# Key buffers of the first batch four deep, half of them in the channel mix's room, with a new order of issue

## The chip, the cores and the metric

One core of a Trainium2 chip runs the whole program. The metric is the time of one execution in device microseconds. The five engines (TensorE or PE, VectorE or DVE, ScalarE or ACT, GpSimd or POOL, SyncE or SP) run their own instruction lists side by side and wait for each other by semaphores; SP's list here is the queue from which all loads, copies and transposes by DMA are issued.

## What is computed

Attention with queries averaged over pairs, then a channel mix (shifted blend, squared ReLU, sigmoid gate) over the attention's output. Shapes: batch 8, heads 8, 1152 keys, head size 64; d_model 512, d_ff 1024.

```python
q_pool = q.reshape(B, H, S // 2, 2, D).mean(axis=3)
scores = scale * np.matmul(q_pool, k.transpose(0, 1, 3, 2))
attn = softmax(scores)                                  # max subtracted, over the keys
x = np.matmul(attn, v).transpose(0, 2, 1, 3).reshape(B, S // 2, H * D)
x_prev = shift(x, 1)                                    # one token back in the sequence
xk = mu_k * x + (1 - mu_k) * x_prev
xr = mu_r * x + (1 - mu_r) * x_prev
out = sigmoid(xr @ w_r) * (np.maximum(xk @ w_k, 0.0) ** 2 @ w_v)
```

## The kernel before, in words

There are 64 heads n (batch n//8, head n%8), and each head's 576 pooled queries are worked on in 6 blocks of 96, so 384 blocks i with n = i//6. All numbers are split into a high and a low half of 16 bits, and products are summed from the halves.

A head's keys take this way (`prep`). They are loaded into kr (L453). ACT makes their high half in kn (L474), POOL the low half (L479; DVE for the first two heads). A transpose by DMA turns kn into ks1, with the high half in partitions 0 to 63 and the low half in 64 to 127 (L482). A copy by DMA then brings ks1's high half to partitions 64 to 127 of ks2 (L485). The other half of ks2 is constant, and set once by memsets at the start (L395, L396). There are two buffers each of kr, kn, ks1 and ks2, taken in turn (n%2). Head 0 is done on PE instead of by transposes. Queries are loaded two heads at a time (L418) and turned by two DMA transposes, one for the high and one for the low half (L443). Values are loaded into vr (L453).

A block is worked on like this (`block`). Nine matmuls of ks1 with the queries' high half (L526, *first scores*) go into a PSUM buffer, s[i%3]. DVE takes the maximum of each query over its nine tiles (L548, *long max*); a matmul with the identity, identb, transposes the result (L551); DVE takes the maximum again (L559, *short max*). In the first 60 blocks a matmul spreads this over the block (L563). ACT writes the negative into a row of the queries' low half (L540). Nine matmuls of ks2 with it (L531, *second scores*) add the low part and subtract the maximum. ACT takes the exponential (L573), POOL makes its low half pl (L535), and PE sums values with it (L613 to L620).

After a batch's 48 blocks its 576 tokens go through the channel mix in tiles of 256 (`ff`): matmuls (L827), ReLU (L854), Square into g32 (L856), its low half gl by POOL (L858), more matmuls, the gate, and the store. The weights are loaded (L706) and split into halves beside the first batch. g32 and gl lie idle until the first tile's Square.

Each engine's order is not the order of the code. Every operation is recorded with what it reads and writes, and at the end `Issue.run` takes, engine by engine, the next operation from the list by a number of a packed table, TURNS. `Issue.gaps` adds spare matmuls of zeros on PE in the early part (L960). The order that results is fixed; the engines still wait for data and free buffers.

Of the kernel before, what the change touches and what calls it, by code (L numbers as in the profile page):

```python
# [13 lines left out]
F32 = mybir.dt.float32  # L14
F16 = mybir.dt.float16
# [40 lines left out]
    "Wp$1da!`$gsp`6(3h1tz<nXvoOyz)@N-}EMwk0EzFde=Qmd!rd&{ad#RR%C9a^e6fEG{>d%VjhwD3wYLr4ky;jZMu>C^t0LDYf<WwRLr<Rq7k+mHK+rwbvC2"
    "g<=tfT)sA6Q&)qUn%Wv<3)y@olg$>hl|oTrgF-r;OQ$o7G8v?E%7SdZkk96F$z&#(P9ixqnN3d0C~7*BMoO)VCX$J0A|8#UBT76OPZC#3FdB`<qQPJ|IK2|="
    "sB~A<PNm|yZd;q%+UmN^s$w^{*-iD$<rbi+mVH2@Q7jee8_hCGjSYIC9_&p{WF}%usfJ>zl&VXmYSOioIR(UXxwx9hqzzToGg>T?N@^SyEgo^Axo9Y&go#(h"
    "a1Fx_$#m+v6OhmtkYvaV2F-w+lX@Uv8;)b>mP`dSTazhV7`5%NY6UG0yB6qDyE;`fpth-MTYFnG6s4(2Yf>6ZC^d5;8XM72wu*&PsiwZZVAR$Yp%?0MT1`!{"
    "uGp$5@JF;hmCR<7$#foxDad5fYAVyO+Ny?lFvj_hgcXN!0#0a#Md3_07-T*G-E~4Chw_@P9%!NXuI@Mvv14*P*(;ISA*$@9nibHXI<{&_HmX`yNHqzhUR86t"  # L60
    "y0lJHH7W#9v)a<42b!7;wXxJ7J!ooTCmQO}(AZF%S_`$VR;{h+*HA#JCY3HCUz1-@ET#*od{QtlT+D!pY$BaTCYw>yM#@mb@wgsSlfhs-9)zld5ecf{kP-||"
    "2nH?14IAACyI{CM_J?Lgx)2J5PPFtu$Or{FH=HUO20dUN%1S$6i)~?7*a6p^6;ZVr)3xCl>XGWOI*p@csFNp~lP9Ta|KQ|)b<#vADs`f_zq7v&TDzvVR-m+_"
    "t*xzdr<O_u9i5$>?R!@$EtL+@m6i^4v^S^??S|T<*Xn9xqY6#Y)EX3X>3lww$`&g{_Lw-Mx+K}z9F?P{m@1@-lZv^*Ag42x&n1y5B#=*J)l5!{Wiq<1E>9X-"
    "+(0y{I^np&tLcQJ3+)KaS142+fiA17(^^*P>h1!i>a=Jdy4v(grMaV1@2r$79h9-XrCjN(pb3?>29dP2Rn-l>Tvn|j2RGYT1C;6&ic~kXE>l~}X&Oiu3aM1C"
    "rY2KN)fP}JCJV{@?0i01n@gtHhrHzTKsK9-$J42fR8Ea&v~)~Y6IwEsNT{J$3<0W*f>_WO--^&a2NwsGATj7T^Cvk+OwuP9gT@4Xa8Mr{(EIg1y?1bMu)C|P"
    "Zvg1;>+h>ndNj4G-|Dm+&D2z*thcpxw5la~o~9;?n$pl(ER}S%uCbV-cB{j=TuohFT~?{7QPB^Io6M%DEcsNfFrOXbT;y_)p--gpMHCC!LS7~GG&P-%Y2j=}"
    "*Mec_$(Rz4Q*|Ovn4q&wCG3Vx!weEsRH9H2Of7IH>65GpmOj8f4DQ4(^y+$FuRho#qVG{rd-~MAUaQkkwMvWH-qGHq8JbQr+M>2JEA<MBC0bTZRa&8CYijb@"
    "VnNN<qLvzhDK*Jlp)g2+3;9g0CRtNNE#)OPGC78%8jIy)NtM<#s$`OCI;E<KfWQM0*zpkkLc~$Qo(M$5GU<BA5fh+0)OOdQ$FWUa2h?iNG*xp|O}Ch~RVbQ5"
    "uRwtK0j92L@bj*2SBoU?2Tgvu??i@n8j>(`XlQq)6bwz7I#pGsOrAVRqdHCC#41X^GKj%}fq|)02L^ik`+NIlp;zha>Fw@8cel!kpV_5!cA}@!-O)9%t7~?5"
    "S4U@u(xITet*y0<utiG?TAG`crg=)aJXmgN)XHj^<JgGS270Xe+WNZMTA*gv+M4}p2?A;ziurtgI);aLnK?WISxn1}Ov6xmXzG+HsxmQ&iHZIRgX#bV(HrfH"  # L70
    "_ICC5^r+nkqoPjh0$M8_E$uGaowhch#cD1oN~8EjO>3wx>Gd@Vlwz)iiYqQIry!F`r?M#(DJ6+SB3c*cC7)<dMB)k+Vjvm^LXk+2CpR1pghHULswF*g#b$+6"
    "Ql)_KAcYe|zhRI?*n_;xWP($mYbpWL($b<dD=p~aNT8`v0{wHjv8SP->^qN!dImJqLEN2O&|DBVSK>6~v&eRccTP{pWGH<SDUmUeK)gAgibbP+aZu7|JkDz<"
    "nk1$oh;)a-!BD%nL2)Zi0CW<ti71nzj{6IJx@9?*z0j}>p(wLSP;|2!26=@hbJwc2DN2hnO&mnImGU<FM5CcRt%*`kZd4i?6l!*D2_k)|Sl>eFQ9BC|et}%J"
    "O*lj*lk1a#R?>-7DupDS24bWO@nmOG`hjpPHV{i75{reSVtZQIg8)^5Lma`1uuI<;h8t9*4<?<$fwoJAMAikv+EYYk7&eWa^r0bOiaJ%9GDVrZe6j#pnShBq"
    "Pn?Je0}}^8MDK!u$pZuEA4CtezK5sYJ}}jVS)Fb45*?lGm9`E*4h1vHEzJ!>O%3HX_M3xHDskTE%^MnOOB4N0E2Ub6^ooQ^sli~e*iYY}AeT#L3z@vYD-VGf"
# [203 lines left out]
def kernel(  # L279
# [40 lines left out]
    def bufs(name, n, shape, dt):  # L320
        return [const.tile(shape, dt, name=f"{name}{i}") for i in range(n)]
# [679 lines left out]
```

## Time and profile before

| | us |
|---|---|
| median of 3 runs (lowest, highest) | 1079.94 (1078.45, 1080.11) |
| profiled execution | 1079.3 |
| its span | 1077.5 |
| PE busy | 1054.2 (98%) |
| DVE busy | 891.2 (83%) |
| ACT busy | 781.0 (72%) |
| POOL busy | 750.1 (70%) |

The granted clock is 1.0 over the span. The busy share of PE counts matmuls with modelled ends, so 98% isn't PE at its peak. The stretch that the key buffers belong to is the first batch, about the first 104 us. The trace's waits are listed by the line that waits and the line that released it; a wait of SP's queue is one of the DMA behind it in the list.

### The profile page before, as it was taken

To read this page: it belongs to the slowest core of one execution; us is meant where nothing else is said; L and a number is where in the kernel's file an instruction comes from. 1 tells how busy PE (TensorE), PEld (TensorE's weight loads), DVE (VectorE), ACT (ScalarE), POOL (GpSimd) and SP (SyncE) were. 2 spreads that over 40 slices of the span, in tenths; PEclk is the share of its full clock that TensorE was granted. 3 is DMA by queue.
4 is the path that set the end of the run, shared out by engine and by line. 5 is a ranking of instruction groups with operands and counts; after the bars stand their busy time and mean duration, and the time that the engine had idled before them with its cause. 6 is when DMAs were issued, how large, how long until landed. Compare 5 with 4: busy or idle time off the path is not lost.

```text
span 1077.5 us, 38432 instructions
## 1 busy us (share of the span) xinstructions
PE 1054.2 (98%) x16153; PEld 867.3 (80%) x16153; DVE 891.2 (83%) x1609; ACT 781.0 (72%) x1523; POOL 750.1 (70%) x748
## 2 busy tenths in 40 slices
PE   8999999999999999999999999999999999999998
PEld 7888878879698888978687978788887879796665
DVE  8999999898978989788779888897988798886331
ACT  7988987777687776777667777777787777665333
POOL 5676778877689676876586886868677876765321
PEclk9999999999999999999999999999999999999999
DMA  9999766764747666665446556547563983521001
GB/s 234 215 241 199 168 166 125 168 131 106 165 94 137 129 128 135 129 127 115 123 95 150 111 115 145 127 94 134 123 155 63 171 157 86 98 47 36 11 20 40
DMA packets 257772, 134.94 MB, mean 125 GB/s; under 512 B 192960, under 2 KB 230080, under 8 KB 257600
## 3 DMA queue, kind: packets, MB, share of 16 engines
q1 hardware_dynamic: 257600, 132.49, 58.2%
q8 instruction: 126, 2.06, 0.8%
q14 instruction: 46, 0.38, 0.1%
HBM read 67.11 MB, written 9.44 MB: 71 GB/s over the span
## 4 chain that ended last, share of the span: by engine, by line
PE 80%; DVE 7%; issue 1%; DMA 1%; POOL 0%; ACT 0%; DVEq 0%; POOLq 0%; ACTq 0%
PE f L827 34%; PE a L613 12%; PE s L526 11%; PE s L531 11%; PE a L620 5%; PE s L827 5%; DVE mx L548 3%; PE s L551 2%; PE a L827 2%; DMA st<-st 1%; DVE mx L559 1%; DVE raw L644 0%; DVE xk L776 0%; DVE xr L776 0%; DVE ex L882 0%
## 5 line engine op out<-in xcount | busy, mean ns | idle before, releaser
L535 POOL TENSOR_SCALAR pl<-pf 128x864 f16<-128x864 uint16 (+1 forms) x384 | 353.7, 921 | 165.3 <-ACT pf L573 135.3
L548 DVE TENSOR_REDUCE mx<-s 128x96 f16<-128x864 f32 x384 | 402.8, 1053 | 53.2 <-PE s L526 31.5
L573 ACT ACTIVATE pf<-s 128x864 int32<-128x864 f32 x384 | 339.7, 888 | 122.7 <-PE s L531 97.7
L613 PE MATMUL a<-vt,pf 128*128 128x129 f16 x2520 | 255.6, 220 | 0.3 <-DVE raw L640 0.3
L531 PE MATMUL s<-qT,ks 128*128 128x96 f16 x3456 | 234.0, 206 | 2.7 <-DMA ks<-ks 1.2
L526 PE MATMUL s<-qT,ks 128*128 128x96 f16 x3456 | 233.7, 206 | 2.3 <-ACT pf L573 1.2
L526 PEld LDWEIGHTS <-ks 128*128 128x128 f16 x3456 | 191.3, 98 | 32.6 <-issue 4.4
L531 PEld LDWEIGHTS <-ks 128*128 128x128 f16 x3456 | 186.4, 98 | 24.3 <-issue 2.2
L620 PE MATMUL a<-vb,pl 128*128 128x65 f16 x2376 | 202.1, 193 | 0.6 <-POOL pl L535 0.6
L613 PEld LDWEIGHTS <-pf 128*128 128x128 f16 x2520 | 176.5, 98 | 27.2 <-issue 0.4
L620 PEld LDWEIGHTS <-pl 128*128 128x128 f16 x2376 | 144.0, 99 | 0.8 <-POOL pl L535 0.8
L540 ACT ACTIVATE qT<-s 1x96 f16<-1x96 f32 x384 | 90.4, 235 | 74.5 <-PE s L551 61.0
L827 PE MATMUL f<-xlk,wk_hi 128*128 128x256 f16 x496 | 135.2, 272 | 0.0
L827 PE MATMUL f<-xhk,wk_lo 128*128 128x256 f16 x496 | 135.1, 272 | 0.0
L827 PE MATMUL f<-xhk,wk_hi 128*128 128x256 f16 x496 | 135.1, 272 | 0.0
L559 DVE TENSOR_REDUCE mx<-s 128x1 f16<-128x128 f32 x324 | 92.8, 286 | 48.3 <-ACT qT L540 46.1
L827 PEld LDWEIGHTS <-wk_hi 128*128 128x128 f16 x1152 | 104.7, 98 | 13.9
L858 POOL TENSOR_TENSOR gl<-g 128x512 f16<-128x512 f32 x72 | 78.4, 1093 | 49.2 <-ACT g L856 46.8
L827 PE MATMUL f<-wv_hi,g 128*128 128x512 f16 (+1 forms) x248 | 92.4, 374 | 1.4 <-ACT em L877 1.4
L479 POOL TENSOR_TENSOR kn<-kr,kn 128x576 f16<-128x576 f32 x62 | 83.7, 1351 | 13.3 <-ACT kn L474 9.7
L827 PE MATMUL f<-wv_hi,gl 128*128 128x512 f16 (+1 forms) x248 | 92.4, 374 | 0.0
L827 PE MATMUL f<-wv_lo,g 128*128 128x512 f16 (+1 forms) x248 | 92.4, 374 | 0.0
(127 smaller groups left out, 1887.3 us busy)
## 6 DMA issues: line engine op xcount, KB each, us to landing
kr<-in_k_dram SPq DMA_DIRECT2D x64, 288.0 KB, 3.5
vr<-in_v_dram SPq DMA_DIRECT2D x64, 288.0 KB, 3.6
qr<-in_q_dram SPq DMA_DIRECT2D x31, 576.0 KB, 5.6
ks<-ks SPq DMA_DIRECT2D x64, 144.0 KB, 3.1
out_dram<-em SPq DMA_DIRECT2D x35, 256.0 KB, 3.4
xt<-in_moe_w_v_dram SPq DMA_DIRECT2D x8, 512.0 KB, 4.7
st<-in_moe_w_k_dram SPq DMA_DIRECT2D x4, 512.0 KB, 6.0
xt<-in_moe_w_k_dram SPq DMA_DIRECT2D x4, 512.0 KB, 6.7
```

Source lines behind the costliest of these rows:

```text
L479: lambda cs=cs, en=nc.vector if ve else nc.gpsimd: en.tensor_tensor(kn[i][:, cs, D:P], kr[i][:, cs], kn[i][:, cs, 0:D], op=ALU.subtract),
L526: nc.tensor.matmul(cols(c, c + 1), ks1[hp][:, c, :], qhi, start=(c == c0), stop=False, skip_group_check=True)
L531: nc.tensor.matmul(cols(c, c + 1), ks2[hp][:, c, :], qlo, start=False, stop=True, skip_group_check=True)
L535: op("POOL", 0.917 if buf == ("pside",) else NC * (r1 - r0) / 1200 + 0.27, lambda: nc.gpsimd.tensor_scalar(to, half(pf, U16, 0)[:, :, HALF ...
L540: op("ACT", 0.131, lambda: nc.scalar.activation(qlo[0:1], src, AF.Prelu, scale=scale, alpha=(1.0 + EPS) / (1.0 - EPS)), r=[("s", at)] + kl ...
L548: op("DVE", 0.974, lambda: nc.vector.tensor_reduce(mxz[:, P - QN:P], grid(0, NC).rearrange("p c q -> p q c"), axis=AX.X, op=ALU.max), r=[( ...
L559: op("DVE", 0.199, lambda: nc.vector.tensor_reduce(to, s[:, 0:P], axis=AX.X, op=ALU.max), r=[("s", z), ("row", z)], w=[("col", z1) if join ...
L573: op("ACT", NC * QN / 1200 + 0.067, lambda: nc.scalar.activation(pf[:, :, HALF + rows.start:HALF + rows.stop], grid(0, NC), AF.Exp, bias=S ...
L613: nc.tensor.matmul(u[:, k_], hi, vt[jv][:, c, 0:D + VN], start=(head and c == 0), stop=last, skip_group_check=True)
L620: nc.tensor.matmul(sum_, pl[:, c, rows], vb[jv][:, c, 0:VN], start=False, stop=(c == NC - 1), skip_group_check=True)
L827: nc.tensor.matmul(ps, terms[i][0], terms[i][1], start=(first and i == 0), stop=(i == last), skip_group_check=True)
L858: op("POOL", 2 * n * 0.0018 + 0.186, lambda f2=f2: nc.gpsimd.tensor_tensor(gl[:, f2, 0:n], g32[:, f2, 0:n], gh[:, f2, 0:n], op=ALU.subtrac ...
```

## The change

In the first batch (n < 8) ks1 and ks2 rotate over four buffers each; from head 8 on over two, as before. The two new ks1 and one new ks2 are parts of g32, read as 16 bit numbers; the other new ks2 is a part of gl. The first tile's Square and its low half are recorded as writing these buffers, so they wait for the last scores that read them. The fixed half of the two new ks2 is set by memsets on POOL, which are operations of the ordered list. The buffers kr, kn, vr and the queries' buffers are as before. The table TURNS is replaced as a whole, so that all five lists change; they hold the same operations but for POOL's memsets and the spare matmuls (98 before, 106 now).

```diff
 TURNS = (
-    "c-nP(2bdhi)$QpVCg-?ec4zZ!-c?+*iYOpJLTiEmArK$~GQogZi~*CQjlf1EVZi)gO!5!b17i$Yg28}DCW)Lxd<X;*0+ISZw`a}wzW2UYHQimQyKhyUd+(|0"
...
+    "c-nP(d7xd>z5i#=!<py#p7EYLoI8(6?#(D6lPRts9)g-<tZ=C*TC;NNp-)AUqMjP6NGs+j^@vLiC26!sL|bV?h!BMRK5L)ouYdgB+Gp>**4k^Yy@t>C^Zl&7"
...
@@ -369,6 +369,17 @@
     g32 = const.tile([P, NF, T], F32, name="g32")
     gl = const.tile([P, NF, T], F16, name="gl")
     r32 = bufs("r32", 2, [P, 2, T], F32)
+    room = [g32.rearrange("p f t -> p (f t)").bitcast(F16)[:, o * NC * P:(o + 1) * NC * P] for o in range(3)]
+    room.append(gl.rearrange("p f t -> p (f t)")[:, 0:NC * P])
+    early_k = [x.rearrange("p (c x) -> p c x", c=NC) for x in room]
+    ks1 += early_k[0::2]
+    ks2 += early_k[1::2]
+    borrowed = [[("ks1", 2, c) for c in (0, 4, 8)] + [("ks2", 2)] + [("ks1", 3, c) for c in (0, 4, 8)], [("ks2", 3)]]
+
+    def slot(n):
+
+        return n % 4 if n < H else n % 2
...
-    for t_ in ks2:
-        nc.vector.memset(t_[0:D], 0.0)
-        nc.vector.memset(t_[0:1].bitcast(F32), SM2)
+    def fixed(t_, en):
+        en.memset(t_[0:D], 0.0)
+        en.memset(t_[0:1].bitcast(F32), SM2)
+
+    for i_, t_ in enumerate(ks2):
+        if i_ < 2:
+            fixed(t_, nc.vector)
+        else:
+            op("POOL", 1.3, lambda t_=t_: fixed(t_, nc.gpsimd), w=[("ks2", i_)], key=-100.0)
...
-            op("DMA", 1.91, lambda: nc.sync.dma_start_transpose(ks1[i], kn[i].rearrange("p c x -> p (c x)")),
-               r=[(m, i, 0) for m in ("kn", "knl")], w=[("ks1", i, c) for c in (0, 4, 8)],
+            op("DMA", 1.91, lambda: nc.sync.dma_start_transpose(ks1[m], kn[i].rearrange("p c x -> p (c x)")),
+               r=[(x, i, 0) for x in ("kn", "knl")], w=[("ks1", m, c) for c in (0, 4, 8)],
                key=key + 1, tail=1.53)
-        op("DMA", 0.95, lambda: nc.sync.dma_start(ks2[i][D:P], ks1[i][0:D]),
-           r=[("ks1", i, c) if n else ("ks1h", c) for c in (0, 4, 8)], w=[("ks2", i)], key=key + 1, tail=1.57)
+        op("DMA", 0.95, lambda: nc.sync.dma_start(ks2[m][D:P], ks1[m][0:D]),
+           r=[("ks1", m, c) if n else ("ks1h", c) for c in (0, 4, 8)], w=[("ks2", m)], key=key + 1, tail=1.57)
...
-                nc.tensor.matmul(cols(c, c + 1), ks1[hp][:, c, :], qhi,
+                nc.tensor.matmul(cols(c, c + 1), ks1[kz][:, c, :], qhi,
...
-                nc.tensor.matmul(cols(c, c + 1), ks2[hp][:, c, :], qlo,
+                nc.tensor.matmul(cols(c, c + 1), ks2[kz][:, c, :], qlo,
...
-                g32[:, f2, 0:n], r32[z][:, :, 0:n], AF.Square), r=[("r32", z)], w=[("g", f0)], key=key + 1)
+                g32[:, f2, 0:n], r32[z][:, :, 0:n], AF.Square), r=[("r32", z)], w=[("g", f0)] + (borrowed[0] if t0 == 0 else []), key=key + 1)
...
-               r=[("g", f0)], w=[("gl", f0)], key=key + 1)
+               r=[("g", f0)], w=[("gl", f0)] + (borrowed[1] if t0 == 0 else []), key=key + 1)
```

Three places of the new order matter below. The lines of the changed kernel have other numbers: L453, L482, L485 and L443 are L470, L499, L502 and L460 there.

The first is SP's list at head 4, whose keys go through kn0 and ks1_0; qT0 is the queries of heads 4 and 5, xt2 a weight's piece. Before:

```order
L482 DMA_TRANSPOSE ks1_0_81<-kn0_79 128x9x128
L453 DMA kr0_73<-in_k_dram 128x576
L706 DMA xt2_110<-in_moe_w_k_dram 128x1024
L443 DMA_TRANSPOSE qT0_85<-qn0_69 128x9x128
L418 DMA qr0_77<-in_q_dram 128x9x128
L443 DMA_TRANSPOSE qT0_85<-qn0_69 128x9x128
L453 DMA vr0_75<-in_v_dram 128x576
L485 DMA ks2_0_83<-ks1_0_81 64x1152
```

And in the changed kernel:

```order
L460 DMA_TRANSPOSE qT0_85<-qn0_69 128x9x128
L435 DMA qr0_77<-in_q_dram 128x9x128
L499 DMA_TRANSPOSE ks1_0_81<-kn0_79 128x9x128
L470 DMA kr0_73<-in_k_dram 128x576
L470 DMA vr0_75<-in_v_dram 128x576
L460 DMA_TRANSPOSE qT0_85<-qn0_69 128x9x128
L502 DMA ks2_0_83<-ks1_0_81 64x1152
```

The weight's piece is gone from between the transpose (first row before) and the copy (last row), and the first query transpose and the query load stand ahead of both.

The second is SP's list at the change from head 7 (kn1, ks1_1; in the changed kernel the parts of g32 and gl) to head 8 (kn0, ks1_0). Before:

```order
L482 DMA_TRANSPOSE ks1_1_82<-kn1_80 128x9x128
L453 DMA kr0_73<-in_k_dram 128x576
L453 DMA kr1_74<-in_k_dram 128x576
L706 DMA xt2_110<-in_moe_w_r_dram 128x1024
L485 DMA ks2_1_84<-ks1_1_82 64x1152
L418 DMA qr0_77<-in_q_dram 128x9x128
L482 DMA_TRANSPOSE ks1_0_81<-kn0_79 128x9x128
```

And in the changed kernel, after head 7's transpose:

```order
L723 DMA xt2_110<-in_moe_w_r_dram 128x1024
L499 DMA_TRANSPOSE ks1_0_81<-kn0_79 128x9x128
L723 DMA xt2_110<-in_moe_w_r_dram 128x1024
L470 DMA kr0_73<-in_k_dram 128x576
L470 DMA kr1_74<-in_k_dram 128x576
L502 DMA ks2_0_83<-ks1_0_81 64x1152
L502 DMA gl_117<-g32_116 64x1152
```

Head 7's copy (the row into ks2_1 before, the row into gl now) has moved behind head 8's transpose and head 8's copy.

The third is POOL's list at the start. Before:

```order
L343 MEMSET qn0_69 128x9x64
masks.py:199 ISA
masks.py:199 AFFINE_SELECT ident_63<-ident_63 128x128
L345 TENSOR_SCALAR negi_71<-ident_63 128x128
L341 CAST identb_68<-ident_63 128x128
```

And in the changed kernel:

```order
masks.py:199 AFFINE_SELECT ident_63<-ident_63 128x128
L406 MEMSET gl_117 64x1152
L345 TENSOR_SCALAR negi_71<-ident_63 128x128
L407 MEMSET gl_117 1x576
L406 MEMSET g32_116 64x1152
L407 MEMSET g32_116 1x576
L341 CAST identb_68<-ident_63 128x128
```

All four new memsets stand ahead of identb, the identity that PE's first transposes read.

## Rows read from the trace of the kernel before

**Rows 1.** The page, busy time of the whole span, and the chain that ended last, by engine.

```profile
PE 1054.2 (98%) x16153; PEld 867.3 (80%) x16153; DVE 891.2 (83%) x1609; ACT 781.0 (72%) x1523; POOL 750.1 (70%) x748
...
PE 80%; DVE 7%; issue 1%; DMA 1%; POOL 0%; ACT 0%; DVEq 0%; POOLq 0%; ACTq 0%
```

**Rows 2.** Busy time by stretch (us from the start, length, then each engine; clock, DMA share, GB/s).

```profile
25.00:50.00 25.00, 23.31 (x567) 21.64 (x564) 23.32 (x42) 22.45 (x43) 16.64 (x18) 1.00 1.09 208
75.00:106.00 31.00, 28.58 (x655) 26.02 (x655) 29.99 (x54) 27.08 (x51) 21.17 (x21) 1.00 1.00 206
```

**Rows 3.** All waits of VectorE, 9 to 106 us (line waited for: us in total, times, longest).

```profile
DVE mb L559 <- PE s L551: 2.0, 4, 1.0
DVE mx L548 <- PE s L526: 1.3, 3, 0.9
DVE mb L559 <- PE s L960: 0.7, 2, 0.4
DVE mx L548 <- ACT qT L540: 0.6, 1, 0.6
```

**Rows 4.** Waits of TensorE, 175 us to the end: the two on maxima.

```profile
PE s L551 <- DVE mx L559: 1.9, 3, 1.1
PE s L551 <- DVE mx L548: 1.5, 3, 0.9
```

**Rows 5.** Waits of TensorE, 0 to 106 us: the one kind on key transfers.

```profile
PE s L531 <- DMA ks<-ks: 1.2, 2, 1.0
```

**Rows 6.** Timeline of TensorE at block 24 (start, length, what, [idle before <-releaser]).

```profile
58.32 0.56 PE L531 MATMUL s<-qT,ks 128*128 128x96 f16 x9 [1.03 <-DMA ks<-ks]
```

**Rows 7.** Timeline of VectorE behind this wait.

```profile
58.97 0.29 DVE L559 TENSOR_REDUCE mb<-s 128x1 f16<-128x128 f32 x1 [0.97 <-PE s L551]
```

**Rows 8.** Wait of SyncE's queue for TensorE, 38.5 to 42.2 us.

```profile
SPq L482 <- PE s L526: 2.7, 1, 2.7
```

**Rows 9.** Timeline of SyncE's queue, head 4's transpose to head 4's copy.

```profile
41.88 1.32 SPq L482 DMA_TRANSPOSE ks<-kn  x1
...
47.62 5.32 SPq L443 DMA_TRANSPOSE qT<-qn  x1
...
53.66 0.47 SPq L485 DMA_DIRECT2D ks<-ks  x1
```

**Rows 10.** Landings of L485's nine key copies, then of L482's nine key transposes, 0 to 106 us.

```profile
DMA to landing us min/median/max: 2.9/5.3/7.1
...
DMA to landing us min/median/max: 3.4/5.3/8.8
```

**Rows 11.** Timeline of GpSimd at the start.

```profile
0.87 0.58 POOL L343 MEMSET qn<- 128x576 f16 x1
...
2.21 0.29 POOL L341 CAST identb<-ident 128x128 f16<-128x128 f32 x1
```

**Rows 12.** Timeline of TensorE at its first use of identb.

```profile
6.38 0.54 PE L436 MATMUL s<-identb,qn 128*128 128x128 f16 x5
```

**Rows 13.** Timeline of VectorE at the start.

```profile
1.20 1.14 DVE L395 MEMSET ks<- 64x576 uint32 x2
```

**Rows 14.** Timeline of TensorE at the last second scores of head 7.

```profile
103.48 0.37 PE L531 MATMUL s<-qT,ks 128*128 128x96 f16 x5
```

**Rows 15.** Timeline of ScalarE at the first Square.

```profile
120.52 0.61 ACT L856 ACTIVATE g<-r 128x512 f32<-128x512 f32 x1
```

**Rows 16.** Timeline of SyncE's queue, head 7's copy and head 8's transpose.

```profile
84.60 0.47 SPq L485 DMA_DIRECT2D ks<-ks  x1
...
87.35 4.21 SPq L482 DMA_TRANSPOSE ks<-kn  x1
```

**Rows 17.** Timeline of GpSimd, low halves of head 8's keys.

```profile
80.68 1.69 POOL L479 TENSOR_TENSOR kn<-kr,kn 128x576 f16<-128x576 f32 x1
```

**Rows 18.** Timeline of TensorE, first second scores of head 7.

```profile
94.71 0.54 PE L531 MATMUL s<-qT,ks 128*128 128x96 f16 x9
```

**Rows 19.** Landing of head 7's copy, issued at 84.60.

```profile
DMA to landing us min/median/max: 6.8/6.8/6.8
```

More of the change, by code (lines that the diff above doesn't have):

```diff
@@ L56 @@
[L56 to L63, printed above, removed]
@@ new lines @@
+    "Y)Pi1>6#Yi%|^)5bv+f(t+1{_hY?C^x~!#CLzOj6)*`y9sj{82<e()Ra==7X*P!ZQ-7qp{(9m_&Fanm!NB}uaG1QpCXKQ&as`(W)s2~~k*&bMulrrp;5%$0g"
+    "m?G$@xNe&8TNaG0t@~I}*tFEBu4fWiRrB~ffNfhD*)(OZY<XfH)AWjlo0<^_8!(L^TW<1}lmSBz_=6l<C1S@Cw%7L9io(vxAroQSG!h&i7LBs7W#+wxs#`h~"
+    "-3;l9t}7vURE0%7VbhikQ`UW!&HMaDSd6O`_UNW+u#0>q2Uq8;$ucB&V~|xzfht!TD{{Fkp~z4w7ONGM8>@||l*&>=v7ykA&qK-;N(HG<K)yB8kjZ4T$fVK@"
+    ">0Cb7fLuck*<>b}NF|ayOPLlH$i(BRcsy}HB7t~Hnwv~#(#cdR8cjsw(aAAHlhFxMT#hH=h{^eAEEtIf!@*EIAcdphXv80ur69o+^m_f?Hg9cmTW6cpF16XV"
@@ new lines @@
+    "-O|$9VmEtiSu(3FRkKi)n)1~W*awueB`s4xsiGFuVljh!F<mGm^2r9Uh4D;7p;(B=V!3=AxmXrRr^B(Z9FHritR|FDJQjc~p&=5q!w4c6uso92YXm$24L;4Q"
+    "YPMG;qCI8JwpGjL^Qk(sG><3Z^=O7=X{zB-J+=zZfhIWfnql~5U6%uz(j|AA9e!D>ar9e_))rZ=pwW=ZQmKS|fg=sD2gQ6T%NfWN3JrRLRs=fpc^Sw?b8K!l"
+    "8!u*J>1Z@M6`5!(8BHJ@lcVt-Sym#DwV)IX*os7(L%=rKx`1x@e7e^=pnE)op6T^^HQ1`B$;&>Nwyjw-E03q%1)^0^M3X(rLRgj}vp<&T13O^bdXHD_>QXzc"
+    "E?boqKF}vOHC3v5qg<(!P-;T83IeKta-m$x%7t8dFrCwKSt2bZWf9Ayo7363>;YrZ=!{e{nayQmu_!>!h$RxT9E+)eNJI|D6@oepPf$Y058bc(Y&O4Nv_U6%"
@@ new lines @@
+    "u%W6Y2HCa=YT8s*_j=Ctu(!78ie@p>d!p*mXey@7j&L3fF$b15!#`b_rc9kKpC(U}r?3~6JaOW{#0iRw-o6RSgh7b`J?KSmPg{3Q>ulB3wl<}!)*?5xp@zn`"
+    "mj1R{bEUQApw^a31+^+lEzPA8r;=l$l*&p`Mpl(+81ZyEO{>V&V)2XsS|*uJ$2f8E_!My|ni3h&6aylOOpQ2{Q<3zES}G-n60)j9)u_)GQer`lX((hEmOm&3"
+    "bid^HX&iy+n%$uu-QG@eYi-lmq*`mORnwZ=)LKn#t<)GQt*xz<N~Nj7D}+{Slibo=Y;MvNQ>~PtWF%EB=fr%)8nTIOLxSiUh-KYoBFSmWWO7Zp+?*UkA|6dQ"
+    "5P)%ZC5}is9Z9E1i;4C`CYp}QNhPet5^^LK3#t*t8&cp2_}OZ&6)^p#FL1CK@RRS|nbRx`3=HV~GX{0FU+wGb>sEVu7OCC+YDaG`divVMv8T63snzt39uBIe"
@@ new lines @@
+    "wyUbQA~)BXRiz-Ku~9;$+)~b!GQ~_KSI(3&nZnePQY>mxK0lbx3r=IJa`8+w6HCR|ABLIf7-=V)$YhX?W+D*d9#2NXaXFUK<b)QNbwqqpL<)y_Ke?DJPR!}L"
+    "LBK(nI_*UjfV0#=Q&s!>W~jaW1EL3$R8{Tn?&$9V8@`~Yt+%U3>6VQa4s@-`v4`4BPgZVjX_ghKk+YdA%h^&<K~p|YR@%EERZNmnrDRTOh;xjyu_RL6WJ$7U"
+    "hA_%TW8iS7l95Cr98b$yQcoyBHA>Emc_okAVA7P|3@Ju{p2-&o1SG%V(`gkFhufojXy$CZCVYo3+$w|vP-ImVN5wEzkraNG?iK8g#oeHHS0pkI<F@K%$Z#D-"
+    "-D$W!gKlK*WK13w;lSZxMkEYR8XA&^q=^%y2`o9#-!J#kn)=bt$sQi!g!lG#OWiZj)!E(I)djhu10C({?bF)PR_m;FbPRTM%<Sx_wb!(oB(=7*5Vp<DO-)Te"
@@ L127 @@
+    "=&VV6_OOGjm38Wdi$_5WlCDU!9EG(?b*%6Cm@Phkxbgo5o%%Fl"
 )
@@ L450, in prep @@
         b, h = divmod(n, H)
-        i, j = n % 2, n % NV
+        i, j, m = n % 2, n % NV, slot(n)
         def dma(o, src, buf, late=0.0):
@@ L506, in block @@
     def block(n, j, i, t):
-        hp, z = n % 2, i % 3
+        hp, z, kz = n % 2, i % 3, slot(n)
         qi = n // 2 % 2
@@ L546, in front @@
                 op("PE", (c1 - c0) * 0.0425, lambda c0=c0, c1=c1: scores(c0, c1),
-                   r=[("ks1", hp, c) for c in (0, 4, 8) if c0 <= c < c1] + kh, w=[("s", z)], key=t)
+                   r=[("ks1", kz, c) for c in (0, 4, 8) if c0 <= c < c1] + kh, w=[("s", z)], key=t)
             op("DVE", 0.974, lambda: nc.vector.tensor_reduce(mxz[:, P - QN:P], grid(0, NC).rearrange("p c q -> p q c"),
@@ L571, in back @@
                 op("PE", (c1 - c0) * 0.0425, lambda c0=c0, c1=c1: scores2(c0, c1),
-                   r=[("ks2", hp)] + kl, w=[("s", z)], key=t + O_EXP)
+                   r=[("ks2", kz)] + kl, w=[("s", z)], key=t + O_EXP)
             op("ACT", NC * QN / 1200 + 0.067, lambda: nc.scalar.activation(
```

123 lines of the change are left out of this document (57 added, 66 removed).

## Prediction, made before the changed kernel was run

> **What bounds the kernel now.** I read first the busy times and the chain of waits, then the busy time of each engine by stretch, then each engine's list of waits in the stretches that the change touches, then the timelines around single waits. The profiled execution took 1079.3 us, 0.64 below the median of the three runs (1079.94). Two of a thousand, 2.16 us, is about what a measurement of this kernel can tell from no change.
>
> Over the whole span TensorE is busy 98%, and 80% of the chain runs over it [rows 1]. That is an average of two stages. From 25 to 50 us DVE and PE are busy alike, 23.3 of 25; from 75 to 106 DVE is busy 29.99 of 31 us and PE 28.58 [rows 2]. So the first batch (blocks 0 to 47, until about 104 us) runs at the pace of VectorE's maxima, and an engine that is late there costs time only if it makes DVE wait. All that DVE waits for between 9 and 106 us adds up to 2.0 + 1.3 + 0.7 + 0.6 = 4.6 us [rows 3]. **This is the ceiling of what new key buffers can give in the first batch.** After it the kernel runs at PE's pace, and PE's waits for maxima there are 1.9 + 1.5 = 3.4 us over 900 us [rows 4].
>
> **The change part by part.**
>
> *1. Heads 2 and 4: the copies ks1 to ks2 come in time.* These are the only key transfers that PE waits for: 1.2 us in two waits [rows 5], 1.03 of them before block 24 [rows 6] and the rest before block 12. The second goes on to DVE, which stands 0.97 us for the transposed maxima behind it [rows 7]; so 1.03 of PE are 0.97 of the bound engine. Why head 4 is late: its transpose into ks1[0] must wait until head 2's last scores have read that buffer (2.7 us of SyncE's queue on PE [rows 8]); it issues at 41.88, and its copy, seven rows behind it, at 53.66, after a query transpose that holds the queue 5.32 us [rows 9]. With slot n%4, head 4 goes into the buffer that head 0 left, so the wait of 2.7 us goes, and the list now puts the copy four rows behind the transpose: of what stood between them, a query load and the first of two query transposes come ahead of both, a weight load goes elsewhere, and the second query transpose stays between. Without the 2.7 alone the copy can issue up to 2.7 us earlier, and it needs 1.03. I take -1.2; bounds 0 (the queue takes the time back) and -1.2 (all of it).
>
> *2. The fixed parts of two more ks2.* Four memsets come onto POOL ahead of identb. The nearest row of POOL is 0.58 us for 576 elements a partition [rows 11]: the two of 1152 cost 2 x 1.16, the two of 576 cost 2 x 0.58, together 3.48 us. identb ends at 2.50 before, at about 5.98 now; PE first reads it at 6.38 [rows 11, 12]. It is hidden by 0.40 us of POOL's idle time, so 0. At DVE's price (two wide pieces in 1.14 [rows 13], so four in 2.28) the margin would be 1.6; if POOL's went by bytes (4 x 1.16) PE would start 0.76 late. Bounds 0 and +0.8.
>
> *3. The room.* Two ks1 and one ks2 lie in g32, the other ks2 in gl, so the first Square of the channel mix and the first gl wait for the scores of heads 2, 3, 6 and 7. The last of these run at 103.48 [rows 14]; the first Square is at 120.52 [rows 15]. 17 us lie between, so 0, and no bound.
>
> *4. Head 7's copy moves the other way.* Before, it stood right behind two key loads and a weight load, and issued at 84.60 [rows 16]. Now it stands behind head 8's transpose and head 8's copy. Head 8's keys are turned only after POOL has their low halves, 80.68 + 1.69 = 82.37 [rows 17]. A transpose lands after 5.3 us at the median, 8.8 at most, and a copy after 5.3, 7.1 at most [rows 10]. At the medians head 8's copy issues at 87.7, head 7's at about 88.2, and it lands at 93.5. PE wants it at 94.71 [rows 18], or 93.5 if term 1 holds. I take 0; the other end is the slowest landings, 82.4 + 8.8 + 0.5 + 7.1 = 98.8, so +5.3.
>
> *5. The order everywhere else.* Each engine's list is new, but with the same operations. On DVE the maxima keep their pace, and in several places of the first batch a short max now precedes a filler (a weight's or a value's piece) that it followed. What this can work on is the 3.4 us of DVE's waits that are left beside term 1 (4.6 - 1.2), and PE's 3.4 after the first batch. Of the latter the largest, 1.1 [rows 4], would move, not go: at block 102 the new list puts the short max ahead of the next long max instead of behind it, so that one is 1.05 us later. I take a third of the first 3.4 and none of the second: -1.1. Bounds: -4.5 (all of the first, a third of the second) and +2, as two waits as long as block 24's come up at places that were tuned in the old list.
>
> The sum: -1.2 + 0 + 0 + 0 - 1.1 = -2.3. From 1079.3 that is 1077.0, and with the 0.64 between profile and median **1077.6 us**.
>
> **The rivals.**
>
> *A. The change does not deliver (1079.0).* The copies come earlier in the list, but SP's queue is what it was: 16 DMA engines are kept busy all through the first batch (share 1.09 and 1.00 [rows 2]), the query transpose that holds the queue 5.32 us still stands ahead of head 4's copy, and the kernel is bound by DVE, where single waits removed come back at the next max. For it: DVE's waits are already under 5% of the stretch. Against it: head 4's transpose loses a definite wait of 2.7. Then terms 1 and 5 give half of 1.2 and about a third of the last: -0.9, so 1079.0, which is no change that can be told.
>
> *B. Head 7's copy becomes the wait (1082.2).* PE would stand at block 42's second scores, and DVE behind it as at block 24. With head 8's transpose landing as late as the slowest (82.4 + 8.8 = 91.2) and head 7's copy at the median (91.7 + 5.3 = 97.0), PE waits 97.0 - 93.5 = 3.5 us: 1079.94 - 1.2 + 3.5 = 1082.2. It decides from 1.2 + 2.16 = 3.4 us of waiting, when head 8's transpose takes over 8.7 us to land, or the copy from 88.2 over 8.7. For it: head 8's transpose stood 4.21 us in the queue before, and head 7's copy took 6.8 to land, over its median [rows 16, 19]; two weight loads now stand on either side of that transpose. Against it: the median landings just fit, and in the list before PE had 3.3 us to spare (84.60 + 6.8 against 94.71). From these rows, one landing of this copy known and slow, one in about five: 0.18.
>
> The Trainium skill (DMA: Bandwidth & Descriptors, section "Queues, rings and completion order") says that a DMA's semaphore write is held until all earlier writes of that DMA engine have landed, those of other queues too. By that rule a copy of 144 KB lands as late as the loads ahead of it, the slowest landings would be the usual ones here, PE would wait 98.8 - 93.5 = 5.3 us, and the time would be 1084.0; that copies land after 5.3 us at the median but after 2.9 at the least [rows 10] agrees with it in part only.
>
> *C. More than that (1073.8).* DVE's waits go altogether (4.6) and 1.5 of PE's after it: 1079.94 - 6.1 = 1073.8. Against it: the list must then be right at every place.
>
> **How the numbers follow.** The forecast has a chance of 0.40 and C 0.06, both faster: 0.46. A has 0.36. B has 0.18, with a late start of PE (part 2) on top in some of it. The predicted time is the forecast's, 1077.6. The range starts at C, 1073.8, and goes up over A to B's own figure, 1082.2. Left out are about half of C (0.03) and the heavier half of B (0.09). Faster than 1077.8 (1079.94 - 2.16) is 0.46; up to 1082.1 (1079.94 + 2.16) it is A's 0.36; slower is B's 0.18.
>
> **What would show it.** Right: no wait of PE on the copy at heads 2 and 4, and none of SP's transposes waiting for PE's scores before 100 us; DVE's waits from 9 to 106 us at some 2.3 us instead of 4.6; the first batch ends about 2 us earlier and the rest runs as long as before. Wrong: a PE wait on the copy at head 7 near 93 us (B); a first identity transpose of PE after 6.4 us (part 2); the first batch as long as before with its DVE waits at other lines (A); or a change in the 970 us after the first batch larger than 1.5 us, which no term of mine holds.

## The result, and the profile after

The changed kernel takes 1087.41 us (median of 6, 1085.04 to 1089.42), the kernel before 1080.03 beside it (1078.28 to 1081.23): 1.0070 times, 95% interval 1.0053 to 1.0087. It is slower by 7.4 us, outside the range given. The profiled execution took 1087.57, its span is 1085.8. First the page: busy time, and the chain that ended last.

```profile
PE 1058.5 (97%) x16161; PEld 868.2 (80%) x16161; DVE 900.8 (83%) x1609; ACT 784.0 (72%) x1523; POOL 754.8 (70%) x752
...
PE 76%; DVE 9%; ACT 2%; issue 1%; ACTq 0%; DVEq 0%
```

Beside [rows 1], PE's share of the chain went from 80 to 76% and DVE's from 7 to 9%. DVE does the same number of operations in 9.6 us more (891.2 before, 900.8 now), and POOL is 4.7 longer, of which the new memsets are 3.2.

What the change was meant to bring about came: the copies are in time. SyncE's queue at head 4 and head 7, and PE at the copies that it had waited for or might have:

```profile
43.46 2.64 SPq L499 DMA_TRANSPOSE ks<-kn  x1
...
50.11 0.47 SPq L502 DMA_DIRECT2D ks<-ks  x1
...
91.56 0.54 SPq L502 DMA_DIRECT2D gl<-g  x1
```

```profile
59.55 0.42 PE L548 MATMUL s<-qT,ks 128*128 128x96 f16 x6
...
98.08 0.29 PE L548 MATMUL s<-qT,gl 128*128 128x96 f16 x3
```

Head 4's copy issues 3.6 us earlier than in [rows 9], lands after 4.4 us at 54.5, and is used at 59.55. Its transpose issues 1.6 us later than there, at 43.46; why is told below, with part 1 of the prediction. Head 7's lands after 5.7 us at about 97.3, 0.8 before PE uses it. No wait of PE on a copy is left in its list for the first 113 us; others stand there:

```profile
PE s L580 <- DVE mb L576: 3.2, 8, 0.9
PE a L637 <- POOL pl L552: 1.4, 1, 1.4
PE s L548 <- issue: 1.4, 1, 1.4
PE s L568 <- DVE mx L565: 1.0, 3, 0.4
...
PE a L637 <- issue: 0.8, 1, 0.8
...
PE a L633 <- issue: 0.6, 1, 0.6
```

And from 175 us to the end, where [rows 4] had 1.9 and 1.5:

```profile
PE s L568 <- DVE mx L565: 4.0, 10, 0.8
PE a L630 <- DVE raw L657: 1.6, 4, 0.8
PE s L568 <- DVE mx L576: 1.3, 2, 0.8
PE f L844 <- ACT ex L892: 1.2, 1, 1.2
PE f L844 <- DVE em L910: 0.8, 1, 0.8
```

The whole list comes to 9.1 us, and that of the kernel before to 5.5: 3.6 apart, which is less than what is lost there. A wait shows in them only from the modelled end of the matmul before, and short ones not at all. An estimate from the starts of PE's matmuls, each pair against the usual distance of such a pair in the kernel before, gives 6.6 us more after 175 us, 5.3 of it at waits that the lists have.

Where the time goes is plainest from the start of the same block's exponential on ACT (from the timelines of L573 and L590) in both kernels:

| block | before | changed | behind |
|---|---|---|---|
| 0 | 12.43 | 13.49 | 1.06 |
| 24 | 58.97 | 60.19 | 1.22 |
| 48 | 107.12 | 109.47 | 2.35 |
| 96 | 232.40 | 234.19 | 1.80 |
| 144 | 354.44 | 357.84 | 3.40 |
| 240 | 610.60 | 615.45 | 4.85 |
| 378 | 969.56 | 977.56 | 8.00 |

In these two profiles about 2 us are lost by the end of the first batch, and 6 more come in small steps over the 850 us after it, where the change touches no buffer: only the order of issue differs there. DVE's waits from 9 to 106 us add up to 7.1 us, where the kernel before had 4.6 [rows 3].

### The profile page after: what moved, and what is told of

Its sections match the earlier page's. It is cut to its first block, busy times and chain, and to the rows that moved or that the text cites. A ratio compares the mean times of both kernels' runs of the same rounds, so it can differ in the third digit from the quotient of the medians.

```text
span 1085.8 us, 38418 instructions
## 1 busy us (share of the span) xinstructions
PE 1058.5 (97%) x16161; PEld 868.2 (80%) x16161; DVE 900.8 (83%) x1609; ACT 784.0 (72%) x1523; POOL 754.8 (70%) x752
## 4 chain that ended last, share of the span: by engine, by line
PE 76%; DVE 9%; ACT 2%; issue 1%; ACTq 0%; DVEq 0%
PE f L844 32%; PE a L630 11%; PE s L543 10%; PE s L548 10%; PE a L637 5%; PE s L844 5%; DVE mx L565 4%; PE s L568 2%; PE a L844 2%; DVE xb L672 1%; DVE raw L661 1%; DVE qn L444 1%; ACT pf L590 1%; DVE mx L576 1%; DVE qs L437 1%
## 5 line engine op out<-in xcount | busy, mean ns | idle before, releaser
L590 ACT ACTIVATE pf<-s 128x864 int32<-128x864 f32 x384 | 339.8, 887 | 131.1 <-PE s L548 114.0
L543 PE MATMUL s<-qT,ks 128*128 128x96 f16 x3240 | 222.7, 206 | 1.0 <-ACT pf L590 0.3
L548 PE MATMUL s<-qT,ks 128*128 128x96 f16 x3240 | 222.7, 206 | 0.5 <-ACT qT L557 0.3
L543 PEld LDWEIGHTS <-ks 128*128 128x128 f16 x3240 | 180.8, 98 | 30.2 <-issue 2.1
L548 PEld LDWEIGHTS <-ks 128*128 128x128 f16 x3240 | 176.1, 98 | 20.5 <-issue 1.2
```

The costliest lines, as they stand in the source:

```text
L543: nc.tensor.matmul(cols(c, c + 1), ks1[kz][:, c, :], qhi, start=(c == c0), stop=False, skip_group_check=True)
L548: nc.tensor.matmul(cols(c, c + 1), ks2[kz][:, c, :], qlo, start=False, stop=True, skip_group_check=True)
L590: op("ACT", NC * QN / 1200 + 0.067, lambda: nc.scalar.activation(pf[:, :, HALF + rows.start:HALF + rows.stop], grid(0, NC), AF.Exp, bias=S ...
```

## The experiments

At block 57 each engine's two lists, old and new, have the same operations behind them. So they can be cut there and joined either way. Theory L put the loss on the lists, in two separate parts, and none on the room; its rivals R (the room costs) and P (what the early part leaves behind makes the late waits) were tried with it.

**The room with the old lists.**

```diff
-TURNS = (the new table)
+TURNS = (the old table; the two new pairs of memsets on POOL right behind identb)
```

> Only the room of the change: four key buffers in the first batch, but all five lists of before (the two new pairs of memsets on POOL behind identb). Theory L (the new lists cost the time, the room nothing): 1079 to 1081 us, as before, perhaps 1 less because head 4's transpose no longer waits 2.7 us on PE; the wait at head 4's copy (1.0) shrinks or goes. Rival R (the room itself costs, by keys that PE reads from g32 and gl or by Square's wait for it): 1083 us or more, and the loss sits in the first batch.

1079.14 us (median of 12) beside 1080.33 (29 runs): 0.9995, interval 0.9982 to 1.0009. The room costs at most 0.1%, and R, which asked for 1083 us or more, falls. The wait on the copies (1.2 us in [rows 5]) is gone from PE's list, but the profile does not show that the room did it. Head 4's transpose issues at 43.69, later than the 41.88 before, and the copy at 52.65, 1.0 earlier; PE itself is 1.0 us behind at block 24, after a stall of 2.0 us that ends at 25.7 and is explained further down. Whether the 1.2 us between the medians is a gain can't be told within this interval.

**New lists early, old lists late.**

```diff
-TURNS = (the new table)
+TURNS = (the new table up to block 57, the old one from there)
```

> The changed kernel up to block 57, then the lists of before (at the cut each engine has the same operations behind it in both lists). Theory L: the loss is in two parts, +2.2 us by block 60 and +5.5 after it from the later lists; so about 1082 us, and from 180 us to the end PE's waits for maxima are those of before (about 3.4 us, not 5.3). Rival P (the later part follows from what the early part leaves behind): 1086 to 1088, with the later waits still there.

1081.17 us, 1.0016 (1.0002 to 1.0030). From 175 us on PE's waits are the old ones again:

```profile
PE s L568 <- DVE mx L576: 1.9, 3, 1.1
PE s L568 <- DVE mx L565: 1.4, 3, 0.9
PE f L844 <- ACT em L894: 1.2, 1, 1.2
PE a L637 <- POOL pl L552: 0.6, 1, 0.6
PE a L630 <- DVE raw L657: 0.3, 1, 0.3
```

In its profile it is 1.17 us behind the kernel before at block 120 and 1.42 at block 360: nothing is lost late. So some 6 of the 7.4 us belong to the late lists, about 1 to the early ones, and the interval of the latter only just leaves out none. P falls.

**Old lists early, new lists late, two buffers.**

```diff
 (the kernel before)
-TURNS = (the old table)
+TURNS = (the old table up to block 57, the new one from there)
```

> The kernel before up to block 57, two key buffers, and the new lists after it. Theory L: 1085 us, +5 to +5.7 against before, all of it after block 60, with PE's waits for maxima at 240, 246, 282, 468, 786 us as in the changed kernel. Rival P: 1080, as before.

1090.19 us, 1.0094 (1.0073 to 1.0114): 9.9 more, without any new buffer. About 3 of it arise where the two tables join (0.29 ahead of the kernel before at block 48, 2.97 behind at block 60, with one wait of 2.16 for a query transpose that ends at 132.38). Behind this wait the granted clock is 0.50, the level of 1.2 GHz, for 3.4 us (the third number from the end of the row below; 1.00 on both sides of it), and a matmul of 256 columns takes 0.41 us there instead of 0.27.

```profile
133.50:136.90 3.40, 3.40 (x35) 3.14 (x33) 1.63 (x3) 2.88 (x6) 2.47 (x3) 0.50 0.11 23
```

From block 144 to 360 it goes from 5.67 to 10.11 behind, and it ends 11.0 behind (spans 1088.5 and 1077.5). After the join it thus loses 8.0 us in its profile, where L had 5 to 5.7; the changed kernel loses 7.2 from block 60 on (1.13 to 8.3). PE's waits from 175 us on are the changed kernel's (4.0 us in ten waits for the long maximum in both). So L holds in its place and not in its size, and the seam was not foreseen.

**SyncE's new list alone, early.**

```diff
-TURNS = (the new table)
+TURNS = (the old table; SyncE's list up to block 57 from the new one)
```

> The room, and of the new lists only SyncE's up to block 57; all else as before. Theory F (in the first batch PE stops because its instructions, which come by DMA in pieces, arrive late behind loads that the new SyncE list issues together): PE's waits without a releaser ('issue') at instructions 711, 1217, 1729, 2243 of PE come to 3 us and more as in the changed kernel (1.5 before), and the time is 1 to 3 us above the room with old lists. Rival D (the early loss comes from the lists of DVE, ACT and POOL, such as the low halves of head 2's keys on POOL beside a DVE piece at 11 us): within 1 us of the room with old lists, PE's waits without a releaser at 1.5.

1079.14 us, 0.9993 (0.9982 to 1.0004), as the room with old lists; PE's waits without a releaser are 1.0 us in one place. F, as put, falls: SyncE's list costs nothing that can be told.

The rival D named a place at 11 us, and the traces bear it out. The first line is DVE's in the changed kernel, the second POOL's there, the third DVE's in the run with the new lists early, which has the same program up to block 57:

```profile
11.28 1.27 DVE L444 SCALAR_TENSOR_TENSOR qn<-qs,qn 128x256 f16<-128x256 f32 x1
```

```profile
11.00 1.27 POOL L496 TENSOR_TENSOR kn<-kr,kn 128x576 f16<-128x576 f32 x1 [5.37 <-ACT kn L491]
```

```profile
10.87 0.41 DVE L444 SCALAR_TENSOR_TENSOR qn<-qs,qn 128x256 f16<-128x256 f32 x1
```

Where DVE comes after POOL's piece has started, its own takes 0.86 us longer, and block 0 starts at 13.49 instead of 12.43. Of the four profiles with this early program three lose about 1.1 us here (13.49 to 13.62) and one nothing. In the lists of before POOL has this piece at 17.14.

**Maxima ahead of long pieces.** The late waits follow a pattern. Here is one of them in the changed kernel, on PE, then on DVE and POOL just before:

```profile
240.52 0.23 PE L568 MATMUL s<-identb,mx 128*128 128x128 f16 x1 [0.81 <-DVE mx L576]
```

```profile
237.85 1.45 DVE L793 SCALAR_TENSOR_TENSOR xk<-xr,mu_k,xt 128x64 f32<-128x64 f32 x1
239.22 1.04 DVE L565 TENSOR_REDUCE mx<-s 128x96 f16<-128x864 f32 x1
240.19 0.28 DVE L576 TENSOR_REDUCE mx<-s 128x1 f16<-128x128 f32 x1
240.39 0.47 DVE L793 SCALAR_TENSOR_TENSOR xk<-xr,mu_k,xt 128x64 f32<-128x64 f32 x2
```

```profile
237.82 1.40 POOL L681 TENSOR_TENSOR st<-xb,st 128x640 f16<-128x640 f32 x1
```

A blend of 64 columns (two of them take 0.47 at 240.39) takes 1.45 us: POOL's piece started 0.03 us before it and ended at 239.22, and the blend ended 0.08 us later. It stood until POOL was through, and the long max, the short max and PE stood behind it. The Trainium skill (Trainium Architecture — The Big Picture, section "What this means for kernel authors") says that DVE and GpSimd share a pair of ports to SBUF that only one of them holds at a time; these rows agree. The maxima read PSUM and keep their 1.05 us beside POOL, as one at 242.77 beside a piece of POOL from 242.90 to 243.81. So, theory C: put the maxima ahead of such pieces.

```diff
 (DVE's list of the changed kernel, 26 moves like this one)
-L793 xk<-xr,mu_k,xt 128x64
 L565 mx<-s (long max)
 L576 mx<-s (short max)
+L793 xk<-xr,mu_k,xt 128x64
```

> The changed kernel with 26 moves in DVE's list after block 70: at 19 places where PE waited 0.26 us or more for a maximum or a sum, the DVE piece ahead of it that took much longer than usual (a blend, a query's or a value's piece that met a POOL operation, 1.0 to 1.5 us for 0.2 to 0.75) now stands behind it. The losses of these places sum to 10 us. Theory C (the late lists cost because DVE pieces that wait for POOL stand ahead of the maxima that PE needs next): 1081 to 1084 us, some of the 10 coming back at other maxima. Rival S (the maxima are late because DVE has no room there at all; what is moved delays the next one as much): 1086 us or more.

1088.41 us, 1.0091 (1.0075 to 1.0108), no better than the changed kernel. DVE is shorter, but PE waits more than before the moves:

```profile
350.00:1075.00 725.00, 715.87 (x10257) 577.62 (x10255) 573.52 (x1039) 498.97 (x973) 494.92 (x488) 1.00 0.51 107
```

```profile
PE s L568 <- DVE mx L565: 5.3, 8, 1.2
```

DVE's 573.52 us are what the kernel before takes for the stretch (572.30, below), and PE is busy 715.87 of 725 where it was 718.33. Over the whole span DVE takes 890.7 us, as in the kernel before (891.2) and 10 less than in the changed one, and yet nothing is won. The waits at 240.52 and 282.47 are gone, and others stand elsewhere, as one of 1.19 us at 372.70 behind a piece (L899) that takes 1.57. C's remedy falls, and with it the reading that the lengthening of DVE's pieces in sum is what counts. That each moved piece makes the next maximum late was not followed piece by piece.

**Without POOL's work.** To see whether POOL is needed for the loss at all, its pieces were cut to a sliver from head 24 on, with the old and with the new late lists. Both leave the low halves out of most columns.

```diff
 (one of POOL's seven kinds of pieces; CUT = 24; the other six alike, left out here)
-                to, half(pf, U16, 0)[:, :, HALF + r0:HALF + r1], LO, 1.0, op0=ALU.mult, op1=ALU.mult),
+                to[:, 0:NC if n < CUT else 1], half(pf, U16, 0)[:, 0:NC if n < CUT else 1, HALF + r0:HALF + r1], LO, 1.0, op0=ALU.mult, op1=ALU.mult),
...
```

> The kernel before; from head 24 on (about 350 us) POOL's seven kinds of pieces (low halves of keys, values, exponentials, blends, squares, and the turned output) do a sliver of their columns, the rest keeps old data; lists as before. Leaves work out, so it is only to be set beside the next run. Theory C: DVE's pieces after 350 us take their usual time, 51 us of lengthening in 200 to 1078 us fall to 10 to 15, and PE's waits for maxima after 350 us (about 2.5) go: 1074 to 1078 us. Rival S: DVE's pieces stay as long, 1079 to 1080.

> The same sliver of POOL's work from head 24 on, with the new lists after block 57 (the kernel that took 1090.2). Before block 144 it is the same program as that, 5.6 us behind the kernel before; from there to the end that one lost another 5. Theory C: with nothing on POOL to wait for, the new lists lose under 1 us after block 144, so 4.5 to 6.5 us above the run with old lists and light POOL. Rival S (the order of DVE and PE alone makes the waits): again about 5 us lost after block 144, 9 to 11 above it.

1076.45 us (0.9978, 0.9964 to 0.9991) with the old lists, 1081.84 (1.0023, 1.0010 to 1.0036) with the new late ones: 5.4 apart, where with POOL's full work it was 9.9. By block:

| block | new late lists behind old, full POOL | light POOL from head 24 |
|---|---|---|
| 96 | 4.05 | 4.01 |
| 144 | 5.67 | 5.07 |
| 240 | 7.21 | 5.15 |
| 360 | 10.11 | 4.76 |

From block 144 on the new lists lose nothing when POOL is light and 4.4 us when it is not, as C forecast for both runs. The row of the stretch 350 to 1075 us, for the kernel before, the changed kernel, and the two with light POOL, old lists and new:

```profile
350.00:1075.00 725.00, 720.43 (x10292) 581.02 (x10289) 572.30 (x1038) 499.56 (x977) 489.97 (x487) 1.00 0.50 106
```

```profile
350.00:1075.00 725.00, 718.33 (x10293) 579.07 (x10291) 582.69 (x1042) 499.83 (x975) 496.57 (x490) 1.00 0.50 107
```

```profile
350.00:1075.00 725.00, 720.72 (x10304) 582.10 (x10303) 537.34 (x1042) 500.71 (x980) 164.90 (x487) 1.00 0.52 107
```

```profile
350.00:1075.00 725.00, 723.31 (x10381) 584.89 (x10379) 541.73 (x1047) 505.67 (x987) 168.11 (x493) 1.00 0.50 107
```

DVE takes 10.4 us more for the new list beside full POOL (582.69 against 572.30; 584.22 with the new late lists alone), and 35 us of its time with the old list and 42 with the new late ones go away when POOL is light. The stretch does not hold quite the same work in each kernel. The whole span does: there DVE takes 891.2 us with the old lists and 899.8 with the new late ones beside full POOL, and 857.3 and 858.4 beside light POOL. That POOL's work is needed for the late loss is shown: with light POOL the new lists of PE, DVE and ACT are all there, and nothing is lost after block 144. That it acts through the standing of DVE is read from the rows at 240 us and others like them, and not shown: the 26 moves took DVE's lengthening away in sum and won nothing, so which pieces count, and how, stays open. PE itself waits for POOL nowhere in the changed kernel after 175 us.

**The early stalls.** PE's waits without a releaser come at fixed places of its own list. Counting all of PE's instructions in the trace from 0, those that wait for semaphores too, they stand at 705, 1217, 1729 and 2241 of the changed kernel, 512 apart. The trace has a DMA queue of its own for instructions, of 16 KB packets:

| stall ends | packet starts | packet ends | PE goes on after |
|---|---|---|---|
| 25.4 | 23.13 | 24.08 | 1.3 |
| 37.6 | 34.67 | 35.99 | 1.6 |
| 50.5 | 48.02 | 49.00 | 1.5 |
| 62.7 | 60.18 | 61.30 | 1.4 |

Packets and crossings alternate every 256 instructions; those between came in time. Each of these four started 3.1 to 3.6 us after PE had begun the 256 instructions before. The last of the four stands in PE's list as a wait for POOL, whose piece was done 0.4 us earlier; in the run below PE passes the same place before POOL has begun this piece. Is it the weights' loads that hold these packets up?

```diff
-lambda s3=s3, src=wv[c, :, f:f + 512]: nc.sync.dma_start(s3, src),
+lambda s3=s3, src=wv[c, :, f:f + 512], late4=iss.nw > 4: nc.sync.dma_start(s3[:, 0:64], src[:, 0:64]) if late4 else nc.sync.dma_start(s3, src),
```

> The changed kernel with the loads of weights after the fourth cut to an eighth of their columns (the rest of the stage keeps old data), so the 16 DMA engines carry 7 MB less between about 35 and 130 us. Theory F (PE stops without a releaser because its own instructions, fetched by DMA, come late behind loads): of PE's waits without a releaser the one at 25 us stays (0.8) and those near 37, 50 and 62 us (1.4, 0.8 and most of the 1.4 that stands by POOL's name) go or fall under 0.3 each; the first batch ends 1.5 to 3 us earlier. Rival N (they have nothing to do with the loads): they stay, 2.8 us and more in the first 110 us.

1085.67 us, 1.0066 (1.0043 to 1.0089), which is not told apart from the changed kernel's 1.0070. PE's waits of this kind:

```profile
PE s L548 <- issue: 1.4, 1, 1.4
...
PE a L637 <- issue: 1.1, 1, 1.1
...
PE a L633 <- issue: 0.6, 1, 0.6
```

The stall at 62 us, which the three other profiles with this early program have, is gone (its packet started 1.26 us after the crossing instead of 3.62); those at 37 and 50 stay. F holds for one of three, by one profile. What holds the other two packets up was not tried.

**PE's list apart from the others.** The stalls at 37, 50 and 62 us stood in the profiles with the new early lists, but for the one at 62 in the run just told. With the old early lists only one of them stood, 0.5 us at 36.91 in the run with light POOL and the new late lists, which the expectation below passes over. So, theory Q: they come with PE's own list.

```diff
 (early lists, up to block 57; late lists old)
-PE, DVE, ACT, POOL, SyncE new
+PE old, DVE, ACT, POOL, SyncE new          (first run; memsets behind identb)
+PE new, DVE, ACT, POOL, SyncE old          (second run)
```

> The room and the new lists up to block 57 for SyncE, DVE, ACT and POOL (the new memsets behind identb); PE's list as before, and all old lists after. Theory Q (the early loss of about 1 to 2 us comes with PE's new list, at the stalls without a releaser near 37, 50 and 62 us, which stood in all four profiles of kernels with that list and in none of the four with the old one): no such stall but the one near 25 us, 1077.5 to 1079.5 us, at or under the room with old lists (1079.1). Rival V (the early lists of DVE, ACT and POOL cost it): 1080.5 to 1082, like all new early lists (1081.2).

> The room and, up to block 57, only PE's new list; all other lists as before. Theory Q: the stalls without a releaser near 37, 50 and 62 us are there again, 2 to 4 us together with the one near 25, and the time is 1 to 2 us above the room with old lists (1079.1): 1080 to 1081.5. Rival V: as the room with old lists, 1078.5 to 1079.5, and no such stalls.

1088.79 us (1.0095, 1.0077 to 1.0112) and 1089.84 (1.0108, 1.0091 to 1.0126). Both theories fall: each mixture loses 8 to 13 us in the first 60 blocks (7.73 and 12.68 behind at block 60), spread over waits of all kinds. With PE's old list:

```profile
PE s L568 <- DVE mx L565: 2.8, 6, 1.1
PE s L543 <- ACT pf L590: 2.2, 6, 0.9
PE s L580 <- DVE mb L576: 2.0, 5, 0.7
PE a L635 <- issue: 1.8, 1, 1.8
```

With PE's new list alone one stall of 1.2 us stands at 40 us and none at 50 and 62; with its old list one of 0.7 stands at 62. What these runs do show is that PE's early list and those of DVE, ACT and POOL can't be taken from different tables, while SyncE's new early list costs nothing by itself. Which of DVE, ACT and POOL must go with PE was not tried.

## Why the prediction was wrong

- **What bounds the kernel.** That the ceiling of the key buffers is 4.6 us of DVE's waits was not contradicted. But it was no floor: these waits were to fall to 2.3 us and rose to 7.1, and block 48 starts 2.35 us later instead of 2 earlier. That the stretch after the first batch runs at PE's pace, and has 3.4 us of waits for maxima to win, was read from the right rows, but only as a gain still to be had. A new list can also lose there, at any of 330 blocks.
- **Part 1, the copies: they came in time, but not by the wait that was to go.** PE's waits on copies are gone. The prediction gave this to the 2.7 us that head 4's transpose no longer waits for PE, and took it that the transpose could start up to 2.7 us earlier. It reads kn's low half too, and POOL had that ready only at 41.45, 0.4 us before the wait for PE ended (first line, the kernel before). With the room and the old lists the transpose starts right behind this piece (second and third line), 1.8 us later than before. In the changed kernel it lands at 50.1, 3.7 us later than before (46.4), and the copy issues at once. What brought the copy forward is SyncE's order: it stands 6.65 us behind the transpose instead of 11.78. No run has this order with two buffers, so whether it needs the room is open. The room with old lists has a median 1.2 us lower, which the interval doesn't tell from none.

```profile
40.17 1.28 POOL L479 TENSOR_TENSOR kn<-kr,kn 128x576 f16<-128x576 f32 x1
```

```profile
42.38 1.28 POOL L496 TENSOR_TENSOR kn<-kr,kn 128x576 f16<-128x576 f32 x1
```

```profile
43.69 1.32 SPq L499 DMA_TRANSPOSE ks<-kn  x1
```

- **Part 2, memsets: right.** They took 1.05 + 0.57 + 1.05 + 0.57 = 3.24 us on POOL for 3.48 worked out; identb was done at 5.63 and first read at 6.46, 0.08 later than before and with no idle time of PE in front of it.

```profile
1.73 1.05 POOL L406 MEMSET gl<- 64x1152 f16 x1
...
3.20 0.57 POOL L407 MEMSET gl<- 1x576 f32 x1
...
5.35 0.28 POOL L341 CAST identb<-ident 128x128 f16<-128x128 f32 x1
```

- **Part 3, the room: right.** The last second scores from gl stand at 106.41, the first Square at 122.65.
- **Part 4 and rival B, head 7's copy: it came in time, in the changed kernel by luck.** Head 8's transpose landed after 5.0 us and the copy after 5.7, near the medians taken. But the transpose issued at 85.92 and not at 82.4, so the copy landed at about 97.3 for 93.5, and PE, late itself, came for it at 98.08 for 93.5: 3.8 and 4.6 us of lateness that happened to cancel. In the five other runs with this part of SyncE's order (new lists early, SyncE's list alone, maxima ahead, light loads, PE's list old) the copy landed 1.7 to 3.8 us before PE used it, so the price of B was paid in none. By the rule of the Trainium skill weighed there (DMA: Bandwidth & Descriptors, section "Queues, rings and completion order") the slowest landings would have been the usual ones; here the nine copies landed after 4.4 us at the median and 6.1 at most.
- **Part 5, the order everywhere else: this is the step that failed.** It took -1.1 with a bound of +2, and looked at one place after the first batch. Measured: about +1 for the early lists (1081.17 against 1079.14 with the same room and old lists makes 2.0, against the kernel before 0.8), and about +6 for the late ones (1087.41 against 1081.17). At block 102 itself the wait did move, as said: PE stands 0.81 us at 240.52 and 0.75 at 245.73 in the place of 1.05. What was missing is a price for the order at all the other blocks. The runs with light POOL point to DVE's pieces beside POOL, though how they act stays open. The wait of 1.05 us at block 102, which the prediction moved as it was, stood behind such a piece, the first line here; the second is this piece in the changed kernel.

```profile
241.58 1.79 DVE L794 SCALAR_TENSOR_TENSOR xlk<-xk,xhk 128x512 f16<-128x512 f32 x1
```

```profile
243.74 0.68 DVE L811 SCALAR_TENSOR_TENSOR xlk<-xk,xhk 128x512 f16<-128x512 f32 x1
```

Before, POOL's piece had started 0.03 us ahead of it (241.55); now POOL's starts 0.15 us behind it, and it is POOL's that is lengthened (1.30 us, 0.91 for the one just before). So the length of this piece came from the order of both lists, and changed with it.

- **The rivals.** The loss went to a case that none of them held. A sentence of the prediction named it as what would prove it wrong: a change of over 1.5 us in the 970 us after the first batch.

## What to carry to other kernels

When a whole table of issue is replaced, price it over the whole program: 2 us of bound is nothing where 300 blocks each have a chance to lose 0.3 to 0.8 us. Read the forms of one operation for their spread of duration, not their mean: a short piece that sometimes takes a microsecond may be standing for another engine, as those at 11 and 240 us here, and no list of waits names it. Before a wait is counted as a gain, look for what would end next: 0.4 us and not 2.7 were to be had at head 4's transpose. Lists tuned together should be kept together; here neither the room with the old lists nor the one with SyncE's new early list (1079.14 us both) is told apart from the kernel before.

## What the runs showed that was not expected

- PE's own instructions come by DMA in pieces of 16 KB, and PE stood for them 0.2 to 2.0 us at a time, one to five times in the first batch, and went on 1.2 to 1.7 us past the end of a packet. The stall of 1.1 us at 24.73 in the kernel before is one. The Trainium skill (Runtime: NRT & Kernel Launch, section "Instruction fetch mechanics") has the blocks of 16 KB and 256 instructions, which agrees, and calls the cost of a crossing mostly hidden. That agrees for most of the 126 packets of the changed kernel; four crossings in its first 63 us were not hidden and cost 0.6 to 1.4 us each.
- Behind some of PE's longest stalls the granted clock is 0.50 for 3.4 us: behind 2.0 us in the run with the room and the old lists, 1.8 in the one with PE's new list alone, and the 2.2 us at the join of the two tables. Behind 1.8 us in the run with PE's old list, and 2.4 in the one with the new late lists and light POOL, it stays at 1.00. So a stall of this length cost more than itself in some runs and not in others.
- With POOL's pieces light for the last 240 blocks, the kernel before is only 0.2% faster (1076.45) though DVE's time in 725 us falls from 572.30 to 537.34: so most of this DVE time was in places where PE had slack.
- The same program's first 24 blocks differ by about 1.2 us from execution to execution (block 24 at 58.95, 59.45 and 60.19 us in three kernels with the same early program), by these fetches and by whether DVE meets POOL's piece at 11 us: 1.06 of the 1.24 between the first and the last stand at block 0 already. A single profile can't price a change of that size there.
